# A layout change in a filter generator: power tables with planes outside and four channel groups innermost, norm blocks between the tables

## The chip, the cores and the metric

The kernel runs on one core of one Trainium2 chip. TensorE (PE) multiplies matrices, VectorE (DVE) and ScalarE (ACT) work element by element, GpSimd (POOL) does small odd jobs, SyncE (SP) issues DMAs. Each engine works through its own queue in order and waits on semaphores for the others. The metric is the device time of one execution in microseconds; the median of several runs counts. A profile is one execution, recorded instruction by instruction.

## The reference, cut to what matters

Two kinds of layer alternate, A, B, A, B, each on a normalised `x` of 2048 rows and 512 channels, each added to `x`. A is an attention with 32 heads in which a row sees itself and seven rows before it, two apart. B is a long convolution per channel:

```python
dt = jnp.exp(log_dt)[:, None]
A = A_re + 1j * A_im                       # (512 channels, 128 states)
Bc = B_re + 1j * B_im;  Cc = C_re + 1j * C_im
logdA = dt * A;  dB = dt * Bc
l = jnp.arange(L).astype(A_re.dtype)       # bf16: many of the 2048 positions fall together
P = jnp.exp(logdA[:, :, None] * l[None, None, :])
K = jnp.einsum("dn,dnl,dn->dl", Cc, P, dB).real
# y = causal convolution of u with K along the sequence, plus u * Dskip
```

With z = exp(dt A), the filter is K[d, l] = Re of the sum over n of C B dt z^l. The positions are rounded to bf16, so only 641 different rows of K are needed. Both B layers use the same K.

## The kernel before, in words

The program first makes K (`k_gen`) and, mixed into it, the first half of the first A layer; then that layer's attention, then the convolution by Fourier transforms, then A and B again without `k_gen`.

`k_gen` writes l = i + b with 32 values i = 0, 8, 16, ..., 248 and 21 values b (`B_L`: 0 to 7, then 256 and up). Then K[d, i + b] = Re of the sum over n of (C B dt z^i)(z^b): for each channel a matrix product over the 128 states. The states lie on the 128 partitions. The 512 channels are four groups g of 128, d = 128 g + q.

- *Squarings* (L761 to L775): z is squared 11 times. ACT squares both planes (`ws`, L764), DVE makes the new real and imaginary part (`sq_z`, L765, L766), ACT copies the power as bf16 into `pow_t` (`Pw`, powers 8 to 128, L768 and L769) or into `B_t` (`Bt`, the other powers, L771).
- *`B_t`* (`bmul`): the remaining z^b are complex products of those, made by `planes_mul` on DVE, in four instructions each (L676, L682, L683, L684).
- *Tables* (`tables(c)`): the channels go in four chunks of 32 values of q (128 channels). For a chunk, `A_t` holds C B dt z^i for the 32 values of i, real and imaginary plane. Row 0 is copied by ACT (L784); each of five levels doubles the number of rows by a complex product with a power from `pow_t`, in three DVE instructions (L676, L679, L680). `A_t` has two buffers.
- *Products*: for each of the 32 values of q, two PE matmuls (real and imaginary plane) with 128 columns of weights (32 i x 4 g, from `A_t`) and 84 streamed columns (21 b x 4 g, from `B_t`) into `pk` (L803); eight values of q fill a PSUM tile, ACT evacuates it into `kgs` (L807). Of the 4 x 4 group pairs the four equal ones are used. After two chunks 24 DMAs on SP write `kgs` to HBM (L821), two chunks later again; `kgs` has one buffer.

In `A_t` and `B_t` a row was a run of 128 elements in the order (g, q), 32 values of q side by side. The 128 weight columns and the 84 streamed columns of one q therefore lay 32 elements (64 bytes) apart.

The *norm blocks* (`front_block`, four of 512 rows) of the first A layer: statistics of four row tiles (two ACT passes each, L75 and L80), a few small DVE and POOL steps (L97 to L102, a power on POOL), the normalised `xn` (L110, DVE), 16 transposes on PE (L167), two ACT copies into `xnT` (L169), 16 projection matmuls for the keys (`pp`, L173), four ACT evacuations into `kT_ext` (L176), and a DVE copy that shifts the keys by one row (`front_ext`, L184). At the end come 16 query projections (`pq`, L132). The sines of the transform (`build_b_consts`, `w_qi`, `w_full`) go in between in steps.

A scheduler sets the order of the instructions on each engine from the program's order and the dependencies. Before, the program's order was: table 0; then for each chunk c: table c + 1, products c, steps of the sines, norm blocks.

Of the kernel before, what the change touches and what calls it, by code (L numbers as in the profile page):

```python
# [11 lines left out]
ALU = mybir.AluOpType  # L12
# [100 lines left out]
class LayerA:  # L113
# [25 lines left out]
    def front_open(self, x_load=None):  # L139
# [3 lines left out]
        self.fp = self.fctx.enter_context(tc.tile_pool(name=f"a{l}_front", bufs=2, side="right"))  # L143
        self.ps_tr = self.fctx.enter_context(tc.tile_pool(name=f"a{l}_ps_tr", bufs=2, space=PSUM, side="right"))
# [10 lines left out]
    def front_block(self, b, x_rows, st_eng, ln_eng, ev_eng, ext):  # L155
        nc, lnst = self.nc, self.lnst
        for a in range(4):
            row_stats(nc, lnst, x_rows[:, a, :], b * 4 + a, st_eng)
        rstd, nb = ln_block(nc, self.fp, lnst, b * 4, b * 4 + 4, st_eng)
        xn = self.fp.tile([P, 4, D], BF16, name="xn")  # L160
# [487 lines left out]
def plane_swap(ap):  # L648

    d = [list(x) for x in ap.ap]  # L650
    st = d[1][0]
    return bass.AP(tensor=ap.tensor, offset=ap.offset + st, ap=[d[0], [-st, 2]] + d[2:])


def k_gen(tc, nc, ident, ins, kd, after_load, after_setup, per_chunk):
# [3 lines left out]
    with ExitStack() as ctx:  # L659
        kgp = ctx.enter_context(tc.tile_pool(name="kg_out", bufs=1))  # L660
        pw = ctx.enter_context(tc.tile_pool(name="kg_pow", bufs=1))
        Bt = pw.tile([P, 2, NB, 4 * P], BF16, name="B_t")
        Pw = pw.tile([P, 3, 5, 4 * P], BF16, name="pow_t")
# [3 lines left out]
        def tmp(shape):  # L667
            t = tmpp.tile([P, 4096], BF16, name="cm_t", tag="cm_t")
            n = 1
            for x in shape[1:]:  # L670
                n *= x
            return t[:, 0:n].rearrange("p (r a b) -> p r a b", r=2, b=shape[3])

        def planes_mul(x, yr, y2, out, signed):
            shape = list(x.shape)
            nc.vector.tensor_tensor(out, x, yr.unsqueeze(1).unsqueeze(1).to_broadcast(shape), ALU.mult)  # L676
            t2 = tmp(shape)
            if signed:
                nc.vector.tensor_tensor(t2, plane_swap(x), y2.unsqueeze(2).to_broadcast(shape), ALU.mult)  # L679
                nc.vector.tensor_tensor(out, out, t2, ALU.add)  # L680
            else:
                nc.vector.tensor_tensor(t2, plane_swap(x), y2.unsqueeze(1).unsqueeze(1).to_broadcast(shape), ALU.mult)  # L682
                nc.vector.tensor_tensor(out[:, 0], out[:, 0], t2[:, 0], ALU.subtract)  # L683
                nc.vector.tensor_tensor(out[:, 1], out[:, 1], t2[:, 1], ALU.add)  # L684

        with ExitStack() as ctx1:
# [10 lines left out]
            nc.vector.memset(Bt[:, 0, 0, :], 1.0)  # L697
            nc.vector.memset(Bt[:, 1, 0, :], 0.0)
            dtb = sp.tile([P, 4 * P], BF16, name="dt_bf")
            nc.scalar.activation(dtb[:].rearrange("p (c g q) -> p c g q", c=NCH, g=4), ldt[:].rearrange("p g (c q) -> p c g q", c=NCH), ACT.Exp)  # L700

            def transposed(name):
                pt = pst.tile([P, 4, P], BF16, name="pt")
                for t in range(4):
                    nc.tensor.transpose(pt[:, t, :], raw[name][:, t, :], ident[:])
                return pt[:].rearrange("p g (c q) -> p c g q", c=NCH)

            def cgq(ap):
                return ap.rearrange("p (c g q) -> p c g q", c=NCH, g=4)
# [3 lines left out]
            nc.vector.tensor_tensor(cgq(a_im), transposed("A_im"), cgq(dtb[:]), ALU.mult)  # L713
            nc.vector.tensor_tensor(cgq(a_re), transposed("A_re"), cgq(dtb[:]), ALU.mult)
# [19 lines left out]
            def c_load(names):  # L734
                for name in names:
                    T[name] = sp.tile([P, 4 * P], BF16, name="in_" + name)
                    nc.scalar.copy(cgq(T[name][:]), transposed(name))
# [10 lines left out]
            def bmul(src, by, dst):  # L748
# [3 lines left out]
                planes_mul(Bt[:, :, s0:s1:st, :], Bt[:, 0, jy, :], Bt[:, 1, jy, :], Bt[:, :, dst:dst + J, :], False)  # L752
# [7 lines left out]
            for k in range(12):  # L760
# [6 lines left out]
                if 3 <= k <= 7:  # L767
                    nc.scalar.copy(Pw[:, 0:2, k - 3], cur[:])  # L768
# [22 lines left out]
        for c in range(NCH):  # L791
            if c + 1 < NCH:
                tables(c + 1)
# [232 lines left out]
```

## Time and profile before

| | |
|---|---|
| median of 3 runs | 562.63 us (559.73 to 563.27) |
| the profiled execution | 563.28 us, span 561.5 us |
| busy PE, DVE, ACT, POOL (share of the span) | 72%, 77%, 63%, 8% |
| last table instruction ends | 142.8 us |
| first matmul of the attention (`L`, L228) | 154.8 us |

Rows of the chain and of timelines give the start in us, the length in us, the engine, the tile that is written, the line and a count. In rows of groups the three numbers after a count are the shortest, middle and longest instruction in ns, or the busy time in us and the mean in ns. A row of the waits names who waited for whom, the sum in us, how often, and the longest. In rows of time windows the busy us of each engine follow with instruction counts in brackets, then the clock granted to PE as a share of full speed. An instruction's length on DVE and ACT overlaps the next one's by some 0.1 us, so sums are made from start to start.

### The profile page before, as it was taken

To read this page: it belongs to the slowest core of one execution; us is meant where nothing else is said; L and a number is where in the kernel's file an instruction comes from. 1 tells how busy PE (TensorE), PEld (TensorE's weight loads), DVE (VectorE), ACT (ScalarE), POOL (GpSimd) and SP (SyncE) were. 2 spreads that over 40 slices of the span, in tenths; PEclk is the share of its full clock that TensorE was granted. 3 is DMA by queue.
4 is the path that set the end of the run, shared out by engine and by line. 5 is a ranking of instruction groups with operands and counts; after the bars stand their busy time and mean duration, and the time that the engine had idled before them with its cause. 6 is when DMAs were issued, how large, how long until landed. Compare 5 with 4: busy or idle time off the path is not lost.

```text
span 561.5 us, 12324 instructions
## 1 busy us (share of the span) xinstructions
PE 405.5 (72%) x5233; PEld 303.0 (54%) x5272; DVE 432.1 (77%) x553; ACT 355.2 (63%) x573; POOL 45.4 (8%) x64
## 2 busy tenths in 40 slices
PE   2013184878999949997967759489998898785595
PEld 1011044746745538675856658244656676585584
DVE  5979996976449999886868765954998988677843
ACT  5999786686327686975758734266552557576532
POOL 1010100110040000002000000610000013200000
PEclk9999665577779958998989979699998999987979
DMA  8000000021022523005768840300025000368403
GB/s 267 23 1 37 37 39 37 39 60 40 37 60 77 139 72 103 12 2 204 265 208 263 275 144 1 76 0 1 21 75 188 2 2 1 131 254 292 153 1 151
DMA packets 31720, 53.19 MB, mean 95 GB/s; under 512 B 11833, under 2 KB 21178, under 8 KB 30386
## 3 DMA queue, kind: packets, MB, share of 16 engines
q1 hardware_dynamic: 29362, 49.79, 27.0%
q10 hardware_dynamic: 2304, 2.62, 1.4%
q8 instruction: 41, 0.67, 0.5%
q14 instruction: 13, 0.11, 0.1%
HBM read 36.57 MB, written 12.19 MB: 87 GB/s over the span
## 4 chain that ended last, share of the span: by engine, by line
PE 42%; DVE 21%; ACT 17%; DMA 8%; issue 4%; POOL 3%; SPq 3%; ACTq 0%; POOLq 0%; DVEq 0%
PE pk L803 6%; PE po L283 5%; PE pq L313 4%; PE pp L173 4%; PE pq L132 3%; PE L L242 3%; PE pb L609 3%; PE pb L610 3%; DMA kf_ring<-kf_dram 3%; DMA kf_dram<-kf_sb 3%; DVE pav L279 2%; SPq L821 2%; PE pb L559 2%; PE pq L296 2%; DVE t L594 2%
## 5 line engine op out<-in xcount | busy, mean ns | idle before, releaser
L239 DVE TENSOR_TENSOR prod<-qT,kT_ext 128x4096 bf16<-128x4096 bf16 x32 | 72.2, 2280 | 17.4 <-PE L L242 14.5
L283 PEld LDWEIGHTS <-pav 128*128 128x128 bf16 x1024 | 64.9, 104 | 17.3 <-DVE pav L279 10.5
L279 DVE TENSOR_TENSOR pav<-attn,v_ext 128x4096 bf16<-128x4096 bf16 x32 | 72.5, 2285 | 1.4 <-DMA v_ext<-v_ext 0.6
L283 PE MATMUL po<-ident,pav 128*128 128x128 bf16 x1024 | 67.9, 230 | 6.0 <-DVE pav L279 6.0
L609 PE MATMUL pb<-Wp,t 128*128 128x128 bf16 x256 | 37.8, 242 | 20.9 <-DVE t L594 18.1
L167 PE MATMUL pt<-ident,xn 128*128 128x128 bf16 x128 | 15.4, 275 | 50.0 <-DVE xn L110 49.9
L173 PE MATMUL pp<-xnT,wqk 128*128 128x512 bf16 x123 | 39.1, 462 | 16.8 <-ACT xnT L169 13.7
L803 PE MATMUL pk<-B_t,A_t 128*128 128x84 bf16 x256 | 42.1, 337 | 11.7 <-DVE A_t L680 10.9
L803 PEld LDWEIGHTS <-A_t 128*128 128x128 bf16 x256 | 37.8, 150 | 15.2 <-DVE A_t L680 12.6
L167 PEld LDWEIGHTS <-xn 128*128 128x128 bf16 x128 | 10.7, 121 | 56.2 <-DVE xn L110 54.8
L593 ACT CAST ub<-pb 128x1024 bf16<-128x1024 f32 x32 | 32.1, 1028 | 11.3 <-DVE t L595 11.0
L609 PEld LDWEIGHTS <-t 128*128 128x128 bf16 x256 | 27.7, 109 | 18.8 <-DVE t L594 18.7
L568 PE MATMUL pb<-a1s,w_sb 128*128 128x64 bf16 x768 | 30.7, 197 | 9.4 <-ACT kf_sb L548 4.2
L242 PEld LDWEIGHTS <-prod 128*128 128x128 bf16 x1024 | 30.5, 97 | 12.5 <-DVE prod L239 4.4
L610 PE MATMUL pb<-WpJ,t 128*128 128x128 bf16 x256 | 37.0, 242 | 0.2 <-DVE t L595 0.2
L548 ACT CAST a1s<-pb 128x1024 bf16<-128x1024 f32 x30 | 30.3, 1017 | 10.7 <-PE pb L559 9.8
L296 PE MATMUL pq<-wop,oT 128*128 128x512 bf16 x111 | 29.7, 380 | 8.2 <-ACT oT L286 7.3
L173 PEld LDWEIGHTS <-wqk 128*128 128x128 bf16 x128 | 14.7, 115 | 38.2 <-issue 31.0
L568 PEld LDWEIGHTS <-w_sb 128*128 128x128 bf16 x768 | 27.1, 100 | 12.3 <-issue 6.9
L242 PE MATMUL L<-ind,prod 128*128 128x8 bf16 x1024 | 31.0, 167 | 3.7 <-DVE prod L239 3.6
L132 PE MATMUL pq<-xnT,wqk 128*128 128x512 bf16 x120 | 31.7, 401 | 1.0 <-issue 0.3
L313 PE MATMUL pq<-wv,xnT 128*128 128x512 bf16 x119 | 30.2, 379 | 0.9 <-ACT qT L134 0.4
(193 smaller groups left out, 941.3 us busy)
## 6 DMA issues: line engine op xcount, KB each, us to landing
kf_ring<-kf_dram SPq DMA_DIRECT2D x64, 256.0 KB, 4.4
w_sb<-w_dram SPq DMA_DIRECT2D x8, 1024.0 KB, 7.0
kf_dram<-kf_sb SPq DMA_DIRECT2D x16, 256.0 KB, 3.4
v_ext<-v_ext SPq DMA_DIRECT2D x6, 448.0 KB, 3.7
wqk<-in_A_wqkv_dram SPq DMA_DIRECT2D x4, 512.0 KB, 6.2
x_sb<-in_A_x_dram SPq DMA_DIRECT2D x4, 512.0 KB, 7.5
w_dram<-w_full SPq DMA_DIRECT2D x4, 512.0 KB, 2.6
w_dram<-w_full ACTq DMA_DIRECT2D x4, 512.0 KB, 2.6
```

The source lines that it names most:

```text
L132: nc.tensor.matmul(pq[:], lhsT=self.wqk[:, dt, ft * P:(ft + 1) * P], rhs=self.xnT[:, dt, q * 512:(q + 1) * 512], start=(dt == 0), stop=(dt ...
L173: nc.tensor.matmul(pp[:], lhsT=self.wqk[:, dt, D + ft * P: D + (ft + 1) * P], rhs=self.xnT[:, dt, b * 512:(b + 1) * 512], start=(dt == 0), ...
L239: nc.vector.tensor_tensor(pr[:], qT[:, ft].unsqueeze(1).to_broadcast([P, W, 4, P]), kap, ALU.mult)
L242: nc.tensor.matmul(L[:, al, w, ft * 8:(ft + 1) * 8], lhsT=pr[:, w, al, :], rhs=ind8[:], start=False, stop=True, skip_group_check=True)
L279: nc.vector.tensor_tensor(pv[:], attn[:, al].unsqueeze(2).to_broadcast([P, W, DH, H]), vap, ALU.mult)
L283: nc.tensor.matmul(po[:, ft, :], lhsT=pvf[:, w, ft * P:(ft + 1) * P], rhs=ident[:], start=(w == 0 and ft == 0), stop=(w == W - 1), skip_gr ...
L296: nc.tensor.matmul(pw[:], lhsT=oT[:, ftp, :], rhs=wo[:, ftp, :], start=False, stop=(ftp == NDT - 1))
L313: nc.tensor.matmul(pp[:], lhsT=xnT[:, dt, a * P:(a + 1) * P], rhs=wv[:, dt, :], start=(dt == 0), stop=(dt == NDT - 1))
L568: nc.tensor.matmul(p2[:, j, :], lhsT=self.w2[:, ec * EC + j, :], rhs=a1s[:, ec * EC + j, :], start=True, stop=True)
L609: nc.tensor.matmul(p3[:, j, :], lhsT=t1[:, dql, :], rhs=wp_r, start=True, stop=False)
L610: nc.tensor.matmul(p3[:, j, :], lhsT=t2[:, dql, :], rhs=wpj_r, start=False, stop=True)
L803: nc.tensor.matmul(o, lhsT=A[:, ri].rearrange("p i (g q) -> p (i g) q", q=CH)[:, :, ql], rhs=Bt[:, ri, :, c * CH * 4 + ql:(c + 1) * CH * 4 ...
```

## The change

1. *Order in memory.* `A_t` becomes [plane, q, i, g] and `B_t` [plane, q, b, g]: the planes outside, the four groups innermost. The 128 weight columns and the 84 streamed columns of one q are now contiguous. Everything upstream is kept in the order (q, g) instead of (chunk, g, q).
2. *Four planes of powers.* `pow_t` holds re, re, -im, im for each chunk and power, where it held re, im, -im. The real plane and the signed imaginary plane are then each one operand over both planes; the swap of the planes moves from the second multiplication to the addition. Each of the five powers takes three ACT copies instead of two.
3. *`B_t` products* take six DVE instructions instead of four: each plane of the source is multiplied on its own.
4. *Order of the program.* table c, then products c - 1, then one norm block, where before it was table c + 1, products c and then one, two or no norm blocks. The statistics of a block come one step ahead of it. `xn` of the first layer has one buffer instead of two.

```diff
-        Bt = pw.tile([P, 2, NB, 4 * P], BF16, name="B_t")
-        Pw = pw.tile([P, 3, 5, 4 * P], BF16, name="pow_t")
+        Bt = pw.tile([P, 2, P, NB, 4], BF16, name="B_t")
+        Pw = pw.tile([P, NCH, 5, 4, 4 * CH], BF16, name="pow_t")
...
+                shape = [P, P, J, 4]
+                x = [Bt[:, r, :, s0:s1:st, :] for r in range(2)]
+                y = [Bt[:, r, :, jy, :].unsqueeze(2).to_broadcast(shape) for r in range(2)]
+                o = [Bt[:, r, :, dst:dst + J, :] for r in range(2)]
+                t2 = tmp(2 * P * J * 4).rearrange("p (r q a g) -> p r q a g", r=2, a=J, g=4)
+                for r in range(2):
+                    nc.vector.tensor_tensor(o[r], x[r], y[0], ALU.mult)
+                    nc.vector.tensor_tensor(t2[:, r], x[r], y[1], ALU.mult)
+                nc.vector.tensor_tensor(o[0], o[0], t2[:, 1], ALU.subtract)
+                nc.vector.tensor_tensor(o[1], o[1], t2[:, 0], ALU.add)
...
-                    nc.scalar.copy(Pw[:, 0:2, k - 3], cur[:])
-                    nc.scalar.mul(Pw[:, 2, k - 3], cur[:, 1], -1.0)
+                    cv = cur[:].rearrange("p r (c x) -> p r c x", c=NCH)
+                    nc.scalar.copy(Pw[:, :, k - 3, 0:2, :], cv[:, 0].unsqueeze(2).to_broadcast([P, NCH, 2, 4 * CH]))
+                    nc.scalar.mul(Pw[:, :, k - 3, 2, :], cv[:, 1], -1.0)
+                    nc.scalar.copy(Pw[:, :, k - 3, 3, :], cv[:, 1])
...
         def tables(c):
-            qs = slice(c * CH * 4, (c + 1) * CH * 4)
-            A = tab.tile([P, 2, NIA, CH * 4], BF16, name="A_t")
-            nc.scalar.copy(A[:, :, 0, :], c0[:, :, qs])
+            A = tab.tile([P, 2, CH, NIA, 4], BF16, name="A_t")
+            A2 = A[:].rearrange("p r q i g -> p (r q) i g")
+            nc.scalar.copy(A[:, :, :, 0, :], c0[:, :, c * CH * 4:(c + 1) * CH * 4].rearrange("p r (q g) -> p r q g", g=4))
             for k in range(5):
                 J = 1 << k
-                planes_mul(A[:, :, 0:J, :], Pw[:, 0, k, qs], Pw[:, 1:3, k, qs], A[:, :, J:2 * J, :], True)
+                shape = [P, 2 * CH, J, 4]
+                y = [Pw[:, c, k, r:r + 2].rearrange("p r (q g) -> p (r q) g", g=4).unsqueeze(2).to_broadcast(shape) for r in (0, 2)]
+                t2 = tmp(2 * CH * J * 4)
+                x = A2[:, :, 0:J, :]
+                nc.vector.tensor_tensor(A2[:, :, J:2 * J, :], x, y[0], ALU.mult)
+                nc.vector.tensor_tensor(t2.rearrange("p (z a g) -> p z a g", a=J, g=4), x, y[1], ALU.mult)
+                o = A[:, :, :, J:2 * J, :].rearrange("p r q a g -> p r q (a g)")
+                half = CH * J * 4
+                sw = bass.AP(tensor=t2.tensor, offset=t2.offset + half, ap=[list(t2.ap[0]), [-half, 2], [J * 4, CH], [1, J * 4]])
+                nc.vector.tensor_tensor(o, o, sw, ALU.add)
...
-                        nc.tensor.matmul(o, lhsT=A[:, ri].rearrange("p i (g q) -> p (i g) q", q=CH)[:, :, ql],
-                                         rhs=Bt[:, ri, :, c * CH * 4 + ql:(c + 1) * CH * 4:CH],
+                        nc.tensor.matmul(o, lhsT=A[:, ri, ql].rearrange("p i g -> p (i g)"),
+                                         rhs=Bt[:, ri, c * CH + ql].rearrange("p b g -> p (b g)"),
...
+        for c in range(NCH + 1):
+            if c < NCH:
+                tables(c)
+            if c > 0:
+                products(c - 1)
+            between(c)
...
+    def between(c):
+        b_steps((4, 4, 6, 100, 0)[c])
+        if c < 3:
+            front0(c + 1)
+        if c < 2:
+            stats0(c + 2)
+        if c < 4:
+            la.front_ext(c, "dve")
+        if c == 3:
+            la.front_q()
```

What the scheduler made of it, at three places. First ACT's queue at the copy of row 0 into the third table's buffer. Before (`A_t_675` is the third table, `kgs_499<-pk_500` the first evacuation of products 0, `w2_full` a sine):

```order
L176 CAST kT_ext_107<-pp_668 128x512
L459 ACTIVATE w2_full_602<-w2_qi_598,w2_sk_368 128x16x32 x4
L807 CAST kgs_499<-pk_500 128x84x8
L807 CAST kgs_499<-pk_518 128x84x8
L460 DMA w2_dram_60<-w2_full_602 128x2048
L807 CAST kgs_499<-pk_536 128x84x8
L807 CAST kgs_499<-pk_554 128x84x8
L784 COPY A_t_675<-c_t_120 128x2x128
```

After (`A_t_781` is the third table; `kgs_617` belongs to products 0, `xnT` to norm block 2):

```order
L804 CAST kgs_617<-pk_618 128x84x8
L804 CAST kgs_617<-pk_636 128x84x8
L462 DMA w2_dram_60<-w2_full_696 128x2048
L804 CAST kgs_617<-pk_654 128x84x8
L804 CAST kgs_617<-pk_672 128x84x8
L456 ACTIVATE w2_qi_704<-w2_base_702,w2_off_384,pk_366 128x256 x2
L171 COPY xnT_102<-pt_728 128x2x512
L171 COPY xnT_102<-pt_738 128x2x512
L75 ACTIVATE ln_junk_91,ln_s1_88<-x_sb_97 128x512
L774 COPY A_t_781<-c_t_120 128x64x4
```

The copy stands behind products 0 as before, and now also behind the two `xnT` copies of norm block 2. Second, DVE's queue where it turns to the third table. Before (`A_t_477` is the second table, `A_t_675` the third):

```order
L679 TENSOR_TENSOR cm_t_492<-A_t_477,pow_t_119 128x2048
L676 TENSOR_TENSOR A_t_675<-A_t_675,pow_t_119 128x2x128
L680 TENSOR_TENSOR A_t_477<-A_t_477,cm_t_492 128x2x1024
L456 TENSOR_SCALAR w2_qi_795<-w2_qi_795 128x512
L676 TENSOR_TENSOR A_t_477<-A_t_477,pow_t_119 128x2x2048
L679 TENSOR_TENSOR cm_t_496<-A_t_477,pow_t_119 128x4096
```

After (`A_t_595` is the second table, `A_t_781` the third):

```order
L781 TENSOR_TENSOR A_t_595<-A_t_595,pow_t_119 128x64x64
L782 TENSOR_TENSOR cm_t_613<-A_t_595,pow_t_119 128x4096
L458 TENSOR_SCALAR w2_qi_704<-w2_qi_704 128x512
L786 TENSOR_TENSOR A_t_595<-A_t_595,cm_t_613 128x64x64
L781 TENSOR_TENSOR A_t_781<-A_t_781,pow_t_119 128x64x4
L782 TENSOR_TENSOR cm_t_783<-A_t_781,pow_t_119 128x256
```

The third table's first multiplication stood ahead of the second table's largest level, and now stands behind all of it. Third, ACT's queue in the squarings, one power of `pow_t`. Before and then after (`ws` is the square, `pow_t` the copies):

```order
L764 ACTIVATE ws_164<-sq_z_263 128x1024
L768 CAST pow_t_119<-sq_z_263 128x2x512
L769 ACTIVATE pow_t_119<-sq_z_263 128x512
L764 ACTIVATE ws_164<-sq_z_269 128x1024
L768 CAST pow_t_119<-sq_z_269 128x2x512
```

```order
L752 ACTIVATE ws_164<-sq_z_269 128x1024
L757 CAST pow_t_119<-sq_z_269 128x4x256
L758 ACTIVATE pow_t_119<-sq_z_269 128x4x128
L759 CAST pow_t_119<-sq_z_269 128x4x128
L752 ACTIVATE ws_164<-sq_z_276 128x1024
```

A third copy stands between one square and the next.

79 lines of the change are left out of this document (28 added, 51 removed).

## The prediction

> **What bounds the kernel now.** The change lies in the first 155 us of the span, where VectorE (DVE) and ScalarE (ACT) are the busy engines. I read first the busy time in four stretches, whose borders I took from the timelines: the squarings, the rest of `B_t`, the tables, and what follows the last table until the attention begins.
>
> ```profile
> core 0: us, PE busy (x) PEld busy (x) DVE busy (x) ACT busy (x) POOL busy (x), PEclk, DMA share, GB/s
> 14.00:43.60 29.60, 2.36 (x16) 1.48 (x17) 25.71 (x47) 28.70 (x52) 2.02 (x3) 1.00 0.03 12
> 43.60:62.60 19.00, 5.25 (x15) 1.74 (x15) 18.94 (x28) 18.87 (x39) 0.39 (x1) 0.91 0.07 28
> 62.60:142.80 80.20, 56.47 (x298) 40.10 (x300) 64.61 (x92) 58.11 (x106) 6.00 (x11) 0.62 0.14 51
> 142.80:154.80 12.00, 11.14 (x68) 9.98 (x70) 4.50 (x2) 3.46 (x5) 0.75 (x1) 0.71 0.00 0
> ```
>
> ACT sets the first stretch (28.70 of 29.6), DVE the second (18.94 of 19.0). In the third DVE works 64.6 of 80.2 us and idles 15.6. In the fourth TensorE (PE) is near full (11.14 of 12.0). Then the chain of waits (start, length, work):
>
> ```profile
> 80.34 10.29 PE pk L803 x64
> 90.66 0.72 ACT kgs L807
> 91.37 0.31 ACT A_t L784
> ...
> 140.55 2.21 DVE A_t L680
> ...
> 144.65 9.35 PE pk L803 x59
> 154.02 0.73 ACT kgs L807
> 154.79 1.01 PE L L228 x2
> ```
>
> A chunk's 64 products (`pk`) last 10.3 us, and after the last table they stand whole between DVE and the attention's first matmul at 154.8. That matmul is the hand-over: the attention's value weights, the second write of the filter and all later stages wait for the same event, so a shift of it goes to the end. Last, DVE's 15.6 us of idling (waiter, awaited, sum, times, longest):
>
> ```profile
> DVE kT_ext L184 <- ACT kT_ext L176: 7.0, 2, 4.2
> DVE A_t L676 <- ACT A_t L784: 4.4, 1, 4.4
> DVE ln_nb L102 <- POOL ln_rstd L101: 3.4, 3, 1.2
> ```
>
> That names 14.8; some 0.8 is small gaps. DVE waits for the norm blocks' keys, for a table buffer still being multiplied, and for the norm's power on POOL.
>
> **The change part by part.** *Squarings.* Each of five powers is copied into four planes instead of three: one more ACT copy of 128x512.
>
> ```profile
> 37.87 0.94 ACT pow_t L768
> 38.81 0.53 ACT pow_t L769
> 39.34 0.95 ACT ws L764
> ```
>
> ACT runs back to back here, so 5 x 0.53 = **+2.65 us**, all on the path. The other copies keep their element counts and now read or write runs of four (8 bytes). The nearest rows: a DVE pass that writes runs of four costs 420 ns against 408 ns contiguous, and ACT reads 2048 elements in runs of four in 1888 ns, twice the 0.94 of 1024 contiguous ones. I take zero.
>
> ```profile
> L110 DVE TENSOR_SCALAR xn<-x_sb,ln_rstd,ln_nb x32: 395/408/5448, 34.8 to 375.2; 128x512 bf16<-128x512 bf16 x32
> L110 DVE TENSOR_SCALAR xnT<-x_sb,ln_rstd,ln_nb x16: 409/420/433, 232.9 to 491.8; 128x512 bf16<-128x512 bf16 x16
> L945 ACT COPY k_perm<-k_rl x4: 1882/1888/1922, 196.9 to 228.5; 128x2048 bf16<-128x2048 bf16 x4
> ```
>
> *`B_t`.* Each complex product goes from four instructions to six: both planes are multiplied apart.
>
> ```profile
> 49.95 0.69 DVE L676 TENSOR_TENSOR B_t<-B_t 128x1024 bf16<-128x1024 bf16 x1
> 50.55 0.69 DVE L682 TENSOR_TENSOR cm_t<-B_t 128x1024 bf16<-128x1024 bf16 x1
> ...
> 51.75 0.42 DVE L683 TENSOR_TENSOR B_t<-B_t,cm_t 128x512 bf16<-128x512 bf16 x1
> 52.09 0.42 DVE L684 TENSOR_TENSOR B_t<-B_t,cm_t 128x512 bf16<-128x512 bf16 x1
> ```
>
> From start to start 1024 elements take 0.60 and 512 take 0.34: two at 0.60 and two at 0.34 make 1.88, six at 0.34 make 2.04, so 0.15 more. Five such products lie in the DVE-bound stretch: **+0.7**. The two before it hide behind ACT (without that cover +0.3).
>
> *Products.* Weights and the streamed operand become contiguous; before, their columns lay 64 bytes apart. The nearest contiguous rows are those of `po`, at a low and at full clock:
>
> ```profile
> 100.26 7.75 PE L803 MATMUL pk<-B_t,A_t 128*128 128x84 bf16 x48 [9.64 <-DVE A_t L680]
> 210.32 6.49 PE po L283 x64
> 248.01 1.79 PE po L283 x32
> 100.20:110.80 10.60, 10.54 (x69) 9.98 (x70) 9.29 (x20) 6.19 (x13) 1.29 (x2) 0.50 0.01 2
> 210.00:217.00 7.00, 6.68 (x65) 6.52 (x67) 6.68 (x10) 3.44 (x7) 0.56 (x1) 0.57 0.19 54
> 248.00:250.00 2.00, 2.00 (x35) 1.84 (x33) 1.81 (x2) 1.57 (x5) 0.00 (x0) 1.00 0.00 0
> ```
>
> A strided product costs 161 ns at clock 0.50 and 9.35/59 = 158 at 0.71: the clock hardly matters to it, so something other than the array sets its pace. A contiguous one, 128 columns wide, costs 101 ns at 0.57 and 56 at 1.00. For 84 columns I scale to 66 and 37 (bounds: no width scaling, 101; no gain, 161). A chunk then takes 4.2 us or 2.4 instead of 10.3.
>
> *Table stage.* DVE's tables keep three instructions per level and all element counts, so its 64.6 us stay; what changes is the idling. I walk down DVE's new queue from the end of table 0 (time zero), with PE at the low clock.
>
> ```profile
> 54.73 1.02 PE L173 MATMUL pp<-xnT,wqk 128*128 128x512 bf16 x4 [0.92 <-ACT kT_ext L176]
> 69.53 1.25 PE L167 MATMUL pt<-ident,xn 128*128 128x128 bf16 x10 [0.53 <-DVE xn L110]
> 71.35 3.57 PE L173 MATMUL pp<-xnT,wqk 128*128 128x512 bf16 x8 [0.57 <-ACT xnT L169]
> ```
>
> ```profile
> 45.73 2.82 ACT w_full L459 x4
> 48.56 1.80 ACT xnT L169 x2
> ```
>
> ```profile
> L676 DVE TENSOR_TENSOR A_t<-A_t,pow_t 128x4096 bf16<-128x4096 bf16 x4 | 9.1, 2287 | 0.1
> L676 DVE TENSOR_TENSOR A_t<-A_t,pow_t 128x2048 bf16<-128x2048 bf16 x4 | 4.9, 1223 | 0.0
> L676 DVE TENSOR_TENSOR A_t<-A_t,pow_t 128x256 bf16<-128x256 bf16 x4 | 1.2, 291 | 4.4 <-ACT A_t L784 4.4
> ```
>
> Rows overlap by 0.09, so from start to start the five levels take 0.20, 0.34, 0.60, 1.13 and 2.20: 4.5, a table 13.4.
>
> - Norm's power: in blocks 1 and 2 only two or three short instructions stand between its request and DVE's use, so the 1.2 us wait stays twice; in block 3 over 6 us of table lie between. 2.4 instead of 3.4.
> - First row of table 2: it needs products 0 done and a copy by ACT. PE has 16 projections (7.1), 64 products (4.2) and block 2's 16 transposes (2.0) ahead, to 13.3; ACT then two `xnT` copies (1.8), a statistic (0.6) and the copy (0.3), to 16.0. DVE arrives at 17.4: table 1 but its first row (13.2), four `xn` (1.3), a key copy (0.6), two index passes (0.7), the norm's wait and its small rows (1.6). The 4.4 us go, with 1.4 us of cover; each us beyond it would come back whole.
> - Keys of block 2: DVE arrives 2.8 later, at 20.2. Block 2's 16 projections start at 15; eight take 3.6, two evacuations 0.5, then a group of sines 2.8 on ACT and the last two evacuations 0.9, to 22.8: a wait of 2.6, as before.
> - Statistics of block 3 alternate with products 1's evacuations, seven ACT pieces of 0.6 after 22.8, to 27.0; DVE arrives at 26.3: a new wait of 0.7.
> - Keys of block 3: from 27.0 DVE has the last 8.1 of table 2 and its small rows, block 3's four `xn` (to 36.8) and table 3 but its last addition with two index passes (11.7): it arrives at 48.5. From 36.8 the transposes (2.0), `xnT` (1.8), eight projections (3.6) and eight more, each four waiting for an evacuation, end at about 47.3 on ACT. The 4.2 us go.
>
> Sum 2.4 + 2.6 + 0.7 and 0.8 of gaps is 6.5 instead of 15.6: **-9.1**.
>
> *Hand-over.* After the last table PE has 64 products, now with eight query projections between them, and one evacuation (0.73). At full clock 2.4 + 8 x 0.255 + 0.7 = 5.1, at half 4.2 + 8 x 0.446 + 0.7 = 8.5. The stretch stood at 0.71, so the middle, 6.8 instead of 12.0: **-5.2**.
>
> ```profile
> 111.49 14.85 SPq L821 DMA_DIRECT2D kd_dram<-kgs x24
> ```
>
> On SP the filter's first half still goes out ahead of a sine group, in 24 issues after products 1, as this row did; the evacuation that reuses their buffer comes some 18 us after products 1 end, behind the 14.85 of the issues and the landing of the last. The statistics only move between ACT rows of like length. The single `xn` buffer waits for transposes that end long before. Both zero.
>
> Sum: 2.65 + 0.7 - 9.1 - 5.2 = -11.0 us. The profiled execution took 563.28 (span 561.5 and 1.8 around it), 0.65 over the median of 562.63: 552.3 in its terms, **551.6** as a median.
>
> **The rivals.** *Runs of four at half rate (slower).* No row of before shows a two-input DVE instruction with rows of four. Its multiplications might take twice as long per element. By the rows of 4096 and 2048 above 2048 elements cost 1.064 us, 0.52 ns each, and would cost as much again. Tables: 2 multiplications x 4 chunks x 7936 elements, 33 us; `B_t` after 43.6: nine columns x 4 x 512, 9.6. That ends at 594. The change turns slower where the multiplications lose over 11/42.6, a quarter, of their rate. Against it speak the 420 ns above, a pass with one input. [...] 12%.
>
> *ACT's queue keeps DVE waiting.* ACT's 58.1 us must fit into 71 instead of 80, in order. If DVE's idling stays 15.6, the third term goes: 561. For it: cover of 1.4 us in one place, and sines, statistics, evacuations and copies in one queue. 12%.
>
> *The clock stays at half.* Shorter products leave PE more idle, and the rows show 0.50 after idle times. The hand-over then takes 8.5, and with the last block's 16 projections in full on the path at +0.19 each, 3 us: 556. [...] 12%.
>
> *The products do not get faster*, their pace being something else than the stride. Then products 0 push table 2 and block 2 by 6 us, and the projections lengthen the hand-over by 2 to 3: 564. 5%.
>
> **How the numbers follow.** The forecast has 59%: its own range is 544 (none of the 5.7 us of waits, full clock at the hand-over) to 556. The range of 543 to 562 takes in the two middle rivals and, below, a part of the ACT delay being hidden; it leaves out the slow runs of four and the last rival, 17%. One per cent, 5.6 us, is about what a measurement here tells from no change: faster than 557 are the forecast, the clock rival and a part of the queue rival, 0.72; within are the rest of it and the last, 0.16; slower the first, 0.12.
>
> **What would show it.** `pk` matmuls 37 to 70 ns apart, not 160; table multiplications of 4096 still at 2.29 us (4.4 or more: the first rival); squarings 2.7 us longer; no DVE wait on the copy into `A_t`, one of 2 to 3 us on keys; first `L` matmul near 144. An `L` matmul there with an unmoved end would show that the hand-over does not carry to the end, and break the whole sum.

## The result, and the profile after

The changed kernel takes 543.62 us (541.74 to 544.80), before in the same set 561.18 (558.75 to 563.27): a ratio of 0.9685, 95% interval 0.9631 to 0.9739. Two later sets gave 0.9644 (0.9614 to 0.9674) and 0.9642 (0.9615 to 0.9669). The forecast was 551.6, so the change brought 8 us more than foreseen. The profiled execution has a span of 541.9 us against 561.5: 19.6 less.

The same four stretches of the changed kernel, busy time by window (columns as in the profile before; the borders are the first `B_t` multiplication after the squarings, the first table instruction, the end of the last table, the first `L` matmul):

```profile
14.00:45.40 31.40, 2.36 (x16) 1.48 (x17) 26.32 (x52) 30.99 (x56) 2.20 (x3) 1.00 0.03 12
45.40:64.30 18.90, 5.58 (x16) 1.91 (x15) 18.90 (x35) 18.90 (x41) 0.39 (x1) 0.94 0.07 28
64.30:131.80 67.50, 29.73 (x296) 18.48 (x296) 64.85 (x95) 56.55 (x104) 10.12 (x11) 0.73 0.17 60
131.80:140.10 8.30, 6.98 (x72) 4.64 (x73) 4.50 (x2) 3.98 (x7) 0.71 (x1) 0.68 0.01 3
```

The tables fell from 80.2 to 67.5 us with the same DVE work (64.85, before 64.61): 15.6 us of idling became 2.65. PE's busy time there halved, from 56.47 to 29.73, and yet its granted clock rose from 0.62 to 0.73. The last stretch fell from 12.0 to 8.3. Of DVE's waits in the tables one kind is left:

```profile
DVE ln_nb L102 <- POOL ln_rstd L101: 2.2, 2, 1.2
```

Timeline rows of PE (start, length, work, idle time before it and its releaser), three of products at the low and the full clock and two of key projections:

```profile
93.72 1.94 PE L175 MATMUL pp<-xnT,wqk 128*128 128x512 bf16 x8 [2.13 <-ACT xnT L171]
96.03 1.89 PE L175 MATMUL pp<-xnT,wqk 128*128 128x512 bf16 x8 [0.38 <-ACT kT_ext L178]
99.53 1.38 PE L800 MATMUL pk<-B_t,A_t 128*128 128x84 bf16 x32 [1.61 <-DVE A_t L786]
...
131.83 2.07 PE L800 MATMUL pk<-B_t,A_t 128*128 128x84 bf16 x27 [3.75 <-DVE A_t L786]
...
138.56 0.76 PE L800 MATMUL pk<-B_t,A_t 128*128 128x84 bf16 x16 [0.51 <-ACT kgs L804]
```

PE's windows around these rows and around the eight query projections after the row at 131.83; then before's, around the eight key projections that I had costed with:

```profile
93.70:97.95 4.25, 3.83 (x16) 1.45 (x15) 4.25 (x4) 3.42 (x7) 0.00 (x0) 1.00 0.01 2
99.50:100.95 1.45, 1.38 (x32) 1.28 (x33) 1.38 (x5) 1.45 (x4) 0.00 (x0) 1.00 0.00 0
131.80:133.90 2.10, 2.07 (x28) 2.02 (x29) 2.02 (x1) 0.84 (x2) 0.00 (x0) 0.50 0.03 12
133.90:137.30 3.40, 3.40 (x15) 1.25 (x13) 2.48 (x2) 0.59 (x1) 0.00 (x0) 0.53 0.00 0
138.55:139.35 0.80, 0.76 (x16) 0.71 (x16) 0.00 (x0) 0.58 (x1) 0.00 (x0) 1.00 0.00 0
```

```profile
71.30:74.95 3.65, 3.57 (x8) 1.14 (x8) 3.62 (x4) 3.65 (x7) 0.00 (x0) 0.50 0.00 0
```

At clock 1.00, 32 products in 1.38 us are 43 ns each, and from the row of 16 to that of 32 each adds 39; at 0.50, after 3.75 us of waiting, 27 in 2.07 are 77. Before, a product took 161 ns at clock 0.50 and 158 in the stretch at 0.71. Eight projections take 1.9 us at 1.00, where the row of before that I had costed with took 3.57 at 0.50. The chain of waits through the hand-over:

```profile
129.58 2.21 DVE A_t L786
...
131.83 2.07 PE pk L800 x27
133.90 3.38 PE pq L132 x8
...
137.30 0.59 ACT qT L134
137.89 0.63 ACT kgs L804
...
138.56 0.78 PE pk L800 x16
...
139.36 0.73 ACT kgs L804
...
140.13 0.59 PE L L230 x2
```

Products are no longer the long piece; eight query projections at 0.42 us each, at a clock of 0.53, are.

The whole difference between the two profiled executions, by borders from the timelines:

| stretch | before | after | difference |
|---|---|---|---|
| start to end of `B_t` | 62.68 | 64.34 | +1.66 |
| to the end of the last table | 80.06 | 67.43 | -12.63 |
| to the first `L` matmul | 12.05 | 8.36 | -3.69 |
| to the first matmul of the transforms (`pb`) | 109.04 | 106.26 | -2.78 |
| to the end | 297.67 | 295.51 | -2.16 |

The first three make -14.66, the shift of the first `L` (154.79 to 140.13). The fourth goes with the clock. PE's windows from the first `L` on, before and after:

```profile
154.80:159.80 5.00, 4.67 (x41) 2.13 (x42) 0.40 (x1) 0.58 (x1) 5.00 (x1) 0.50 0.51 128
```

```profile
140.10:145.10 5.00, 4.97 (x51) 2.47 (x51) 2.11 (x1) 1.76 (x3) 5.00 (x1) 1.00 0.55 128
```

Before, the attention began at the half clock (0.50), after, at the full one (1.00).

### The profile page after: what moved, and what is told of

Read it like the earlier page. It is cut to its first block, busy times and chain, and to the rows that moved or that the text cites. A ratio compares the mean times of both kernels' runs of the same rounds, so it can differ in the third digit from the quotient of the medians.

```text
span 541.9 us, 12380 instructions
## 1 busy us (share of the span) xinstructions
PE 376.7 (70%) x5272; PEld 277.1 (51%) x5272; DVE 432.6 (80%) x567; ACT 356.9 (66%) x578; POOL 49.8 (9%) x64
## 4 chain that ended last, share of the span: by engine, by line
PE 37%; DVE 35%; ACT 13%; DMA 6%; issue 4%; POOL 4%; SPq 1%; DVEq 0%; POOLq 0%; ACTq 0%
PE po L285 6%; PE pq L315 4%; PE pq L132 3%; DVE A_t L781 3%; PE L L244 3%; DVE cm_t L782 3%; PE pp L175 3%; DVE A_t L786 3%; PE pb L611 3%; PE pb L612 3%; DMA kf_dram<-kf_sb 3%; DVE t L596 3%; DVE pav L281 2%; PE pq L298 2%; DVE t L597 2%
## 5 line engine op out<-in xcount | busy, mean ns | idle before, releaser
L169 PE MATMUL pt<-ident,xn 128*128 128x128 bf16 x128 | 14.5, 263 | 57.0 <-DVE xn L110 57.0
L175 PE MATMUL pp<-xnT,wqk 128*128 128x512 bf16 x128 | 36.2, 432 | 18.4 <-ACT xnT L171 16.1
L169 PEld LDWEIGHTS <-xn 128*128 128x128 bf16 x128 | 9.6, 114 | 62.2 <-DVE xn L110 60.5
L298 PE MATMUL pq<-wop,oT 128*128 128x512 bf16 x128 | 33.3, 380 | 6.8 <-ACT oT L288 6.8
L570 PE MATMUL pb<-a1s,w_sb 128*128 128x64 bf16 x768 | 31.8, 199 | 8.1 <-ACT kf_sb L550 3.8
L611 PEld LDWEIGHTS <-t 128*128 128x128 bf16 x256 | 27.8, 110 | 17.4 <-DVE t L596 17.3
L315 PE MATMUL pq<-wv,xnT 128*128 128x512 bf16 x128 | 31.3, 378 | 0.4 <-ACT qT L134 0.4
L317 ACT CAST v_ext<-pq 128x512 bf16<-128x512 f32 x32 | 18.3, 587 | 17.8 <-PE pq L315 17.8
L612 PEld LDWEIGHTS <-t 128*128 128x128 bf16 x256 | 27.9, 110 | 4.2 <-issue 3.3
```

Of the source, the lines that this page charges most:

```text
L175: nc.tensor.matmul(pp[:], lhsT=self.wqk[:, dt, D + ft * P: D + (ft + 1) * P], rhs=self.xnT[:, dt, b * 512:(b + 1) * 512], start=(dt == 0), ...
L298: nc.tensor.matmul(pw[:], lhsT=oT[:, ftp, :], rhs=wo[:, ftp, :], start=False, stop=(ftp == NDT - 1))
L315: nc.tensor.matmul(pp[:], lhsT=xnT[:, dt, a * P:(a + 1) * P], rhs=wv[:, dt, :], start=(dt == 0), stop=(dt == NDT - 1))
L570: nc.tensor.matmul(p2[:, j, :], lhsT=self.w2[:, ec * EC + j, :], rhs=a1s[:, ec * EC + j, :], start=True, stop=True)
L611: nc.tensor.matmul(p3[:, j, :], lhsT=t1[:, dql, :], rhs=wp_r, start=True, stop=False)
L612: nc.tensor.matmul(p3[:, j, :], lhsT=t2[:, dql, :], rhs=wpj_r, start=False, stop=True)
```

## The experiments

Theory: the contiguous operands make the gain, directly (shorter products) and by the clock that PE is then granted. First rival: the new program order makes it, by taking DVE's waits away. Second rival: the products are shorter, but the clock plays no part.

**Layout alone.** The changed kernel in before's program order.

```diff
-        for c in range(NCH + 1):
-            if c < NCH:
-                tables(c)
-            if c > 0:
-                products(c - 1)
+        tables(0)
+        for c in range(NCH):
+            if c + 1 < NCH:
+                tables(c + 1)
+            products(c)
             between(c)
...
-        b_steps((4, 4, 6, 100, 0)[c])
-        if c < 3:
-            front0(c + 1)
...
+        b_steps(6)
+        for b in ((1,), (2, 3), (), ())[c]:
+            front0(b)
+            la.front_ext(b - 1, "dve")
...
```

> The changed kernel's layout, planes of powers and instructions, in the program order of before (table c + 1, then products c, then norm blocks 1, then 2 and 3; statistics inside their block); only the single xn buffer is kept, because memory has no room for two. Theory (contiguous operands carry most of the gain): a product takes 37 to 70 ns, the copy into the third table's buffer is not waited for (4.4 us in before), the last-table-to-first-L stretch falls from 12.0 to 5 to 8.5, and against it the powers' extra copies cost 1.7 as in the changed kernel; the waits on the keys (7.0 in before) shrink but stay, since their order is before's. Time 547 to 554. Rival (the order carries the gain, the layout next to nothing): 558 to 563, with products shorter but DVE idling some 15 us in the tables as in before.

545.99 us, ratio 0.9728 (0.9699 to 0.9757). DVE's waits from the first table to the hand-over (the second falls behind the last table), then three rows of PE and ACT at the hand-over, then PE's window after the first `L`:

```profile
DVE ln_nb L102 <- POOL ln_rstd L101: 3.4, 3, 1.2
DVE w_qi L457 <- ACT w_qi L455: 1.7, 1, 1.7
```

```profile
135.57 1.38 PE L799 MATMUL pk<-B_t,A_t 128*128 128x84 bf16 x32 [1.55 <-ACT kgs L803]
...
136.00 2.95 ACT L460 ACTIVATE w_full<-w_qi,w_sk 128x512 bf16<-128x512 int32 x4
...
140.23 1.01 PE L229 MATMUL L<-maskrow,rows 1*128 1x512 bf16 x2 [3.28 <-ACT kgs L803]
```

```profile
140.10:145.10 5.00, 4.87 (x42) 2.11 (x42) 2.29 (x1) 0.66 (x2) 2.98 (x1) 0.50 0.67 204
```

The key waits are gone without the new order, which no theory had; that shorter products alone do this, the run with contiguous reads below shows. The last table ends at 131.67 (changed kernel 131.77) and the first `L` comes at 140.23 (140.13). The 8.6 us hand-over is of another kind: a sine group on ScalarE stands between the last evacuations, and PE idles 3.28 us. It then begins the attention at the half clock (0.50), and the stretch from `L` to the transforms takes 109.79 us instead of 106.26. So against this kernel the new order is worth what differs after the first `L`, 3.5 us by this stretch, and nothing ahead of it.

**Order alone.** Before's layout and arithmetic, the new order.

```diff
-        tables(0)
-        for c in range(NCH):
-            if c + 1 < NCH:
-                tables(c + 1)
...
+        for c in range(NCH + 1):
+            if c < NCH:
+                tables(c)
+            if c > 0:
+                products(c - 1)
+            per_chunk(c)
...
```

> Before's layout and arithmetic (strided operands, three planes, planes_mul) in the changed kernel's program order: table c, products c - 1, one norm block, statistics one step ahead, one xn buffer. Theory (contiguous operands carry most): products still take about 160 ns, a chunk 10.3 us, and now stand on PE ahead of each norm block's transposes and projections, and after the last table 10.3 of products, 8 query projections at 0.446 and an evacuation make a hand-over of about 14.5 us instead of 12.0; granted clock in the tables stays near 0.5 to 0.6. Time 556 to 566. Rival (order carries): the key and buffer waits go all the same, 545 to 552.

558.80 us, ratio 0.9976 (0.9955 to 0.9997). PE rows of the first and last products and DVE's waits in the tables:

```profile
80.62 10.30 PE L803 MATMUL pk<-B_t,A_t 128*128 128x84 bf16 x64 [2.22 <-DVE A_t L682]
...
141.84 10.31 PE L803 MATMUL pk<-B_t,A_t 128*128 128x84 bf16 x64 [0.90 <-DVE A_t L682]
```

```profile
DVE kT_ext L186 <- ACT kT_ext L178: 4.9, 1, 4.9
DVE ln_nb L102 <- POOL ln_rstd L101: 3.8, 3, 1.3
DVE w_qi L458 <- ACT w_qi L456: 3.1, 2, 2.8
DVE ln_veps L99 <- ACT ln_junk L80: 2.2, 2, 1.7
```

A product stays at 161 ns. The wait for the table buffer (4.4) is gone, others came: 14.0 us of waits against 15.0 before. The hand-over is 11.2, not the 14.5 that I expected, since the query projections were done ahead of the last products. The first rival falls: the order alone brings 0.2%.

**Contiguous reads alone, and the two operands apart.** Before, with other addresses in the products' reads and nothing else; the second and third kernel change one line each. The filter that these three kernels compute is another one; only their times are of use.

```diff
-  lhsT=A[:, ri].rearrange("p i (g q) -> p (i g) q", q=CH)[:, :, ql],
-  rhs=Bt[:, ri, :, c * CH * 4 + ql:(c + 1) * CH * 4:CH],
+  lhsT=A[:, ri, 16 + ql % 16],
+  rhs=Bt[:, ri, ql % NB, 0:84],
```

> Before unchanged but for what the products read: the weights are one row of 128 contiguous elements of the last level of A_t, the streamed operand 84 contiguous elements of a row of B_t; the filter's values are therefore others, every instruction, size, wait and place in the order is as in before. Theory: a product takes 37 (full clock) to 70 ns (half), a chunk 2.4 to 4.5 us, the 4.4 us wait of the third table goes, the hand-over falls from 12.0 to 5 to 7, and the granted clock between 62 and 155 us rises from 0.62 to above 0.75, because busy strided products seem not to raise it and contiguous ones do; the start of the attention then runs at full clock and gains another 2 to 3 us. Time 545 to 551. Rival A (the stride is not what sets 160 ns): 161 ns, 561. Rival B (products shorter, clock not raised, PE being idle more): 66 to 70 ns throughout, clock 0.5 to 0.6, no gain after the first L matmul: 550 to 554.

> As the run with contiguous reads, but only the weights are contiguous (one row of A_t); the streamed operand keeps its 64-byte stride. The filter's values are others. If the weight load sets the 160 ns: a product falls to 37 to 70 ns and the time to that of the run with both contiguous. If the streamed operand sets it: still about 160 ns and 561 us. If each costs part: between, 100 to 130 ns.

> Before with only the streamed operand contiguous (84 elements of a row of B_t); the weights keep their 64-byte stride. The filter's values are others. With contiguous weights alone a product kept 147 ns. If the streamed operand alone sets the pace: 37 to 70 ns and the time of the run with both contiguous, 537 to 540. If the strided weight load has a pace of its own just below: 100 to 150 ns, 552 to 559. The clock: if it is the strided stream that keeps the granted clock at half while PE is busy, the row of 100 to 110 us rises from 0.50 above 0.7.

Both contiguous: 537.20 us, ratio 0.9575 (0.9542 to 0.9608), faster than the changed kernel and below the expected 545 to 551. Weights alone: one execution of 558.01, before's set 557.73 to 562.60. Streamed operand alone: one execution of 541.20, before's set 559.28 to 565.82. PE rows and windows of each, both first:

```profile
133.73 1.39 PE L803 MATMUL pk<-B_t,A_t 128*128 128x84 bf16 x32 [0.27 <-ACT kgs L807]
...
135.93 0.59 PE L228 MATMUL L<-maskrow,rows 1*128 1x512 bf16 x2 [0.81 <-ACT kgs L807]
```

```profile
131.20:136.00 4.80, 3.71 (x69) 3.09 (x70) 4.50 (x2) 3.17 (x5) 0.82 (x1) 1.00 0.00 0
```

The weights alone:

```profile
99.77 7.06 PE L803 MATMUL pk<-B_t,A_t 128*128 128x84 bf16 x48 [9.64 <-DVE A_t L680]
```

```profile
99.70:110.30 10.60, 10.53 (x78) 9.26 (x79) 9.29 (x20) 7.04 (x14) 1.29 (x2) 0.50 0.01 2
```

The streamed operand alone:

```profile
95.88 2.46 PE L803 MATMUL pk<-B_t,A_t 128*128 128x84 bf16 x32 [9.64 <-DVE A_t L680]
...
133.53 3.82 PE L803 MATMUL pk<-B_t,A_t 128*128 128x84 bf16 x59
```

```profile
99.00:106.00 7.00, 4.60 (x51) 3.73 (x52) 6.93 (x12) 6.95 (x12) 0.39 (x1) 0.81 0.26 88
132.30:138.00 5.70, 4.99 (x67) 4.59 (x69) 4.50 (x2) 3.36 (x5) 0.59 (x1) 1.00 0.00 0
```

With strided weights a product takes 77 ns in the row after 9.64 us of waiting (32 in 2.46) and 65 at clock 1.00 (59 in 3.82); with a strided stream 147 at 0.50 (48 in 7.06); with both 161 at 0.50; with neither 43 in a row of 32 at 1.00. So the streamed operand's addresses set the pace. The weights' stride costs 14 ns beside a strided stream at 0.50, 22 beside a contiguous one at 1.00, and next to nothing in the row after the wait, since the changed kernel has 77 after its own wait too, at 0.50. The two are not alike: the 128 weight columns lay 64 bytes apart throughout, the 84 streamed columns only in fours, and the next four followed 1024 bytes on, since a row of `B_t` held the 512 elements of all chunks. Which of these two steps makes the stream slow, no run tells apart.

The same rows decide on the clock. With a strided stream (and contiguous weights) PE is busy for 10.53 of 10.60 us and its granted clock stays at 0.50. With a contiguous stream (and strided weights) it is busy for 4.60 of 7.00 us in that part of the program and is granted 0.81. With both contiguous, DVE's waits in the tables fall from 15.0 to 3.7 us, in before's program order:

```profile
DVE ln_nb L102 <- POOL ln_rstd L101: 3.7, 3, 1.2
```

The first `L` comes 18.9 us earlier than before with both contiguous, and the stretch from `L` to the transforms takes 106.23, as in the changed kernel (109.04 before). The second rival falls.

What contiguous reads would bring if they came without a new layout is thus more than the change brings: the first `L` comes 4.2 us ahead of the changed kernel's. Of these, 3.6 are the hand-over (4.8 instead of 8.4, with four query projections in it instead of eight, and at a clock of 1.00 instead of 0.68) and 0.6 the end of the tables.

**Three planes.** The changed kernel without the fourth plane's copy; its tables hold other values.

```diff
-                    nc.scalar.copy(Pw[:, :, k - 3, 3, :], cv[:, 1])
...
-                y = [Pw[:, c, k, r:r + 2].rearrange("p r (q g) -> p (r q) g", g=4).unsqueeze(2).to_broadcast(shape) for r in (0, 2)]
+                y = [Pw[:, c, k, r:r + 2].rearrange("p r (q g) -> p (r q) g", g=4).unsqueeze(2).to_broadcast(shape) for r in (0, 1)]
```

> The changed kernel without the fourth plane of powers: the third copy of each of the five powers is left out, and the table multiplications read planes that lie there already (re, -im instead of -im, im), with the same shapes; the tables' values are others. Prediction's price: ACT sets the squarings, so all five copies are on the path and the tables start 2.65 us earlier, at 61.6 instead of 64.25. What the trace of the changed kernel suggests: the start of the first multiplication of 128x3072 (1536 now) moved only 1.7 later than before, so part was hidden: the tables start 1.5 to 1.8 earlier, at 62.5 to 62.8. Third possibility (the copies are hidden and the delay comes from the copies' runs of four): no move.

541.60 in one execution. The first `B_t` multiplication after the squarings with three planes, and then in the changed kernel:

```profile
44.35 0.96 DVE L737 TENSOR_TENSOR B_t<-B_t 128x1536 bf16<-128x1536 bf16 x1 [0.24 <-ACT B_t L760]
```

```profile
45.38 0.96 DVE L737 TENSOR_TENSOR B_t<-B_t 128x1536 bf16<-128x1536 bf16 x1 [0.24 <-ACT B_t L761]
```

The five copies cost 1.0 us, not 2.65 and not 1.7. Before's start is 43.66; the other 0.7 remains without them. The tables start at 63.23, so all three figures that I had put down were off. Why only 1.0, one row of ACT's timeline shows, of before, of the run with three planes and of the changed kernel:

```profile
36.81 1.06 ACT L764 ACTIVATE ws<-sq_z 128x1024 f32<-128x1024 f32 x1 [0.83 <-DVE sq_z L766]
```

```profile
37.51 1.06 ACT L752 ACTIVATE ws<-sq_z 128x1024 f32<-128x1024 f32 x1 [0.86 <-DVE sq_z L754]
```

```profile
37.49 1.06 ACT L752 ACTIVATE ws<-sq_z 128x1024 f32<-128x1024 f32 x1 [0.27 <-DVE sq_z L754]
```

ACT does wait once among the squarings: DVE works norm block 0 into them. The first three copies fall ahead of that row, which starts at the same time without them. Of their 1.6 us the wait took 0.6, and 0.7 is a statistics pass (L75) that stands ahead of the row in the other two kernels and comes later in the changed one. The last two copies, 0.52 each from start to start, fall behind the row, where ACT is back to back.

**Sine groups earlier.** In the changed kernel the last query projections fell into the hand-over because their evacuations stood behind a sine group and two evacuations of products on ScalarE, whose timeline there is:

```profile
126.81 2.93 ACT L461 ACTIVATE w_full<-w_qi,w_sk 128x512 bf16<-128x512 int32 x4 [0.56 <-DVE w_qi L458]
129.65 0.69 ACT L804 CAST kgs<-pk 128x672 bf16<-128x672 f32 x1
...
130.24 0.71 ACT L804 CAST kgs<-pk 128x672 bf16<-128x672 f32 x1
130.85 1.06 ACT L134 CAST qT<-pq 128x512 bf16<-128x512 f32 x2
```

Two kernels move the sines: the changed one, and the one with before's order.

```diff
-        b_steps((4, 4, 6, 100, 0)[c])
+        b_steps((6, 6, 100, 0, 0)[c])
```

```diff
-        b_steps(6)
+        b_steps((8, 100, 0, 0)[c])
```

> The changed kernel with the steps of the sine groups given as 6, 6, all instead of 4, 4, 6, all: the last sine group leaves ScalarE's queue ahead of the fourth table's end, so that the 16 query projections are evacuated, and stand on PE, before the last 64 products instead of 8 of them between. Theory (in the hand-over the 8 query projections at the low clock cost 3.6 of 8.4 us, and they are there because their evacuations stood behind a sine group): last table to first L falls to 3.4 to 5.0 us, first L at 135 to 137, time 538 to 541. Rival 1 (earlier sines delay statistics, evacuations and the copies of row 0, and DVE waits in the tables again): the fourth table ends 2 to 3 us later, time 542 to 545. Rival 2 (PE, idle for longer before the products, runs them at half clock): hand-over 5 to 5.5, 540 to 542.

> The run with the changed layout in before's program order, with the sine steps 8, all instead of 6 for each chunk. In that run a sine group of 2.95 us stood on ScalarE between the last evacuations and held the first L to 8.6 us after the last table. Theory (order of before is as good as the new one for this layout, and the sine group was what cost it): hand-over 3.5 to 5, first L at 135 to 137, time 539 to 542, level with the changed kernel's order with early sines. Rival (the new order has a worth of its own, in the statistics and key waits): the fourth table ends 2 us or more later than 131.7, time 543 to 546.

541.29 us, ratio 0.9645 (0.9580 to 0.9710), and 539.67, ratio 0.9611 (0.9551 to 0.9672). The last table addition and the first `L`, for the first and for the second kernel:

```profile
131.85 2.29 DVE L786 TENSOR_TENSOR A_t<-A_t,cm_t 128x4096 bf16<-128x4096 bf16 x1
...
138.47 0.59 PE L230 MATMUL L<-maskrow,rows 1*128 1x512 bf16 x2 [0.81 <-ACT kgs L804]
```

```profile
130.85 2.29 DVE L785 TENSOR_TENSOR A_t<-A_t,cm_t 128x4096 bf16<-128x4096 bf16 x1
...
137.08 0.59 PE L229 MATMUL L<-maskrow,rows 1*128 1x512 bf16 x2 [0.81 <-ACT kgs L803]
```

The hand-over fell as expected, from 8.4 to 4.3 and 3.9. But the fourth table ends 2.4 and 1.4 us later, as the first rival had it for a part. The first `L` gains 1.7 and 3.1. Before's order is no worse than the new one once the sine group is out of the way.

**The fourth plane by POOL, and the repeats.** The kernel with before's order and early sines, now with the fourth plane's copy on POOL; then that kernel again as it was, and the changed kernel again beside each.

```diff
-                    nc.scalar.copy(Pw[:, :, k - 3, 3, :], cv[:, 1])
+                    nc.gpsimd.tensor_copy(Pw[:, :, k - 3, 3, :], cv[:, 1])
```

> The run with the changed layout, before's program order and early sines, and the fourth plane of each power copied by POOL instead of ScalarE. Theory (the fourth copy costs 1.0 us, as the run with three planes showed, and POOL's copy stands beside the squarings): the tables start 1.0 earlier, near 63.3, first L near 136, time 538 to 540, 0.5 to 1.5 under the run without POOL's copies. Rival (POOL takes over 2 us for a copy, and the norm's powers, which wait behind three of them on POOL, or the tables' first levels wait for the planes): tables or norm blocks start later, DVE waits on ln_rstd grow from 3.7, time 540 to 544.

> The changed kernel as it is, once more, beside the run with early sines and POOL's copies, so that the two stand against the same runs of before: 542 to 545, ratio near 0.9685; the other 3 to 5.5 us below it. If it comes out within 1 us of the other, the gain of the variants is within what differs between sets of runs.

> The run with the changed layout, before's program order and early sines, once more with more rounds, since its first interval (0.9551 to 0.9672) overlaps that of the changed kernel (0.9614 to 0.9674). If its first L matmul, 2 to 3 us ahead of the changed kernel's, carries to the end: ratio 0.958 to 0.961. If what follows the attention takes the lead back: 0.963 to 0.966.

> The changed kernel beside it, against the same runs of before: ratio 0.9644 as in its last set, 0.962 to 0.968.

POOL's copies brought nothing: 540.39 us, ratio 0.9641 (0.9604 to 0.9678), tables starting at 64.17 as with ScalarE. The row of DVE's waits on POOL:

```profile
DVE sq_z L752 <- POOL pow_t L758: 1.0, 2, 0.5
```

DVE now waits 1.0 us for POOL, as much as ScalarE's copies had cost. That this wait alone takes the gain back was not tested.

The changed kernel came to 541.62 and 541.40 in these two sets, the early sines to 540.26 (0.9628, 0.9591 to 0.9665). The intervals overlap, so no version beats the changed kernel by what these runs can tell. The first `L` does come earlier each time (137.45 and 137.08 against 139.42 to 140.13), but what follows the attention differs more than that between executions: from the transforms' first matmul to the end, eight profiled executions of kernels with the changed layout took 293.1 to 296.3 us, and a ninth, the repeat of the early sines, 299.1. Why was not found.

## Why the prediction was right or wrong

- *Squarings, +2.65:* 1.0. The step "ACT runs back to back here" was true of the three rows quoted and not of the whole stretch: the first three copies were covered by one wait of 0.83 us, before the fourth power, and by a statistics pass that moved behind the squarings.
- *`B_t`, +0.7 in the DVE-bound stretch and nothing ahead of it:* the stretch is 18.96 us long against 19.02, but before it held the first multiplications of two tables (at 57.10 and 59.71) and an index pass of 0.34, so +0.7 stands. The two products ahead of it were not covered: 0.7 of the 1.7 us by which the stretch begins later stays without the fourth plane, and 0.3 of that is these two products (DVE is 0.41 late ahead of them and 0.68 behind them), the +0.3 that the prediction had given without cover. The other 0.4 is there before 14 us, and its cause is open. Both terms together were forecast at +3.35 and came to +1.66.
- *Products, 66 and 37 ns:* 77 and 39 to 43; the scaling by columns held but for the low clock, 17% over (77 at 0.50, the 66 scaled from a row at 0.57). The stride was the cause, as forecast; that it is the stream's and hardly the weights', the prediction had not said.
- *Tables, -9.1:* -12.6, the largest miss. The norm waits came as forecast (2.2 for 2.4), and so did the two waits said to go. The wait on block 2's keys (2.6) and that on statistics (0.7) did not come, and the gaps shrank from 0.8 to 0.45. The step that failed is "with PE at the low clock". Counted from the end of table 0, at 82.1, DVE came to the copy of block 2's keys at 20.6, close to the walk's 20.2, but the keys were there at 19.1 instead of 22.8. Almost all of this was won before block 2's projections, which began at 11.6 instead of 15: from 86 to 97 us PE had the full clock (1.00, after 0.51 from 82 to 86), and did the projections, products and transposes ahead of them in 9.5 us, not 13.3. Block 2's own projections then took 1.9 us per eight (at 1.00), not 3.57 (at 0.50). Layout alone has no key waits either, so the new order was not what decided.
- *Hand-over, -5.2:* -3.7. The mechanism held, 8.36 us instead of 6.8, at the half-clock bound of 8.5: PE had waited 3.75 us for the last table, and its clock was 0.50 for the first products and 0.53 for the eight projections. The 0.71 from which the middle was taken was no middle clock: it was 1.00 at first and 0.50 from 148 us on.
- *The shift carries to the end unchanged:* at least that. The first `L` moved by 14.7, the transforms by 17.4, since the attention began at the full clock (1.00, before 0.50). The stretch between was 105.7 to 106.3 us in ten of the profiled executions of this study, the changed kernel's among them, and 108.2 to 109.8 in the other four, among them before's and that of layout alone, which both began the attention at 0.50. The last 2.2 us lie within the spread of the rest.
- *Rivals.* Runs of four at half rate: gone, the multiplication of 4096 elements takes 2288 ns (the row below) against 2287. ACT's queue holding DVE: no wait on ACT is left in the tables. Products not faster: gone. *The clock stays at half* is the one that had something: it held in the hand-over (0.50 and 0.53), and was the wrong way round elsewhere (0.73 against 0.62 in the tables, 1.00 against 0.50 at the start of the attention). I took a PE with less to do for one with a lower clock.

```profile
L781 DVE TENSOR_TENSOR A_t<-A_t,pow_t 128x4096 bf16<-128x4096 bf16 x4 | 9.2, 2288 | 0.0
```

The direction was right for its first reason, the stride. The size was some 8 us short, above all because the clock was taken as a given, where it was one of the things that the change moved. Between the two profiled executions 8.6 us are missing from the forecast: 3.5 in the tables, most of it by the clock, and 2.8 in the attention by the clock, less 1.5 at the hand-over; 1.7 are the squarings and `B_t`, and 2.2 lie within the spread of the rest. The time came out at the low end of the range, 543, and below the 544 that the forecast allowed itself. The range went that far down for a part of the ACT delay being hidden, which came true with 1.7 us; the gain behind the first `L` was not foreseen, so that the range holds is in part luck.

## What to carry to other kernels

Where a matmul's pace does not follow the granted clock (161 ns at 0.50, 158 in a stretch at 0.71), look at the addresses of the streamed operand first: here columns in fours, 64 bytes apart, with 1024 bytes from one four to the next, cost a factor of 1.9 (147 ns against 77, at 0.50) to 2.4 (158 against 65 in the hand-over), and the clock besides (0.50 at its end against 1.00). When a change takes such a stall away, cost the neighbours at both clocks, since the projections next to it also halved (3.57 us per eight at 0.50, 1.9 at 1.00). And look which engine's queue holds the evacuations at the point where one stage hands to the next: what is moved out of there has to go somewhere, and here a third to six tenths of the gain at the hand-over came back in the tables.

## What was unexpected in the hardware

In these runs a PE that the profile shows as busy was not always granted its full clock. Before, 10.54 of 10.60 us were busy at a granted 0.50; with contiguous weights and a strided stream 10.53 of 10.60, at 0.50 again; with a contiguous stream 4.60 busy of 7.00 us went with 0.81. The busy time alone thus does not tell the granted clock; what does was not tested. The prediction read the first of these rows as a 0.50 after idle time; it held through 10.6 us of work as well.

Nor did a 0.50 need a wait like the 9.64 us ahead of that row. Before's last 59 products begin at 144.49 at the full clock, and some 3.3 us later the granted clock halves, with PE busy all the time:

```profile
144.60:147.60 3.00, 3.00 (x21) 2.85 (x20) 2.75 (x2) 1.30 (x2) 0.00 (x0) 1.00 0.00 0
147.40:147.80 0.40, 0.40 (x5) 0.38 (x4) 0.00 (x0) 0.00 (x0) 0.00 (x0) 1.00 0.00 0
147.80:148.20 0.40, 0.40 (x5) 0.39 (x3) 0.00 (x0) 0.00 (x0) 0.00 (x0) 0.53 0.00 0
148.00:154.00 6.00, 5.99 (x38) 5.43 (x37) 0.00 (x0) 1.44 (x2) 0.00 (x0) 0.50 0.00 0
```

The products come at the same pace on both sides: from start to start 157 ns apart up to 147.8 us and 159 after it, on the mean. With a contiguous stream the same stage keeps the full clock (1.00, the row 132.30:138.00 above). With the strided stream the clock falls while the products run, and before's attention begins at 0.50.
